# Transform pieces of the last five batches placed by tables of steps, with each piece's PSUM bank written down

## The chip, the cores and the metric

The kernel runs on one core of one Trainium2 chip. A core has five engines with queues of their own: TensorE (PE in the profile; its weight loads are PEld), VectorE (DVE), ScalarE (ACT), GpSimd (POOL) and SyncE (SP), which here only issues DMAs. The metric is the device time of one execution in microseconds (us). Before the change the median of three runs is 810.65 us (809.49 to 811.81).

## What is computed

Each of 8 batches has 3008 rows of 256 channels. A real Fourier transform along the rows, a multiplication with a complex filter and the inverse transform mix the rows; then each row goes through a layer of 2048 hidden channels with a leaky activation that has a slope of its own for each hidden channel.

```python
X = np.fft.rfft(x, axis=1)                      # x: 8 x 3008 x 256
F = (filt_r + 1j * filt_i)[None, :, :]
y = np.fft.irfft(X * F, n=x.shape[1], axis=1)
...
h = y.reshape(24064, 256) @ w_in                # 256 -> 2048
g = np.maximum(h, 0.0) + alpha * np.minimum(h, 0.0)
out = g @ w_out                                 # 2048 -> 256
```

## The kernel before

**The layer.** The rows of a pair of batches (6016) are cut into 12 blocks of 512 (the sixth has 384), so there are 48 blocks, and each has 16 steps: 768 steps, 96 for a batch. In each step PE does the up product of one group of 128 hidden channels (two matmuls of 512 columns, L414, into one half of a double PSUM tile hps) and one sixteenth of the down product of the block before (four matmuls of 256 columns, three behind the 384 block, L433). After every second step ACT moves both halves of hps to SBUF (gtb, L420), and DVE makes the activation of it in place (two L423, one L424). After every eighth step (phases 7, 15, ... 71, 79, ... of a batch's 96) ACT moves two finished down results to osb (L438), and SP stores them with two or three DMAs (L396).

**The transform.** It is split in two factors, 3008 = 47 x 64, and done by small pieces that are put between the steps. For one batch b there are

- 16 pieces A: one matmul of 512 columns (L164), moved by ACT to asb (L238). After every fourth one save_a lets SP store a quarter of asb to DRAM (a_dram, L169). turn_a then loads all of it back in another layout, as at (four DMAs in steady state, L176; their lines of DRAM are 512 bytes).
- 12 pieces B: two matmuls (L184) from at. DVE reads their PSUM tile twice, with two copies of the filter (ww L188, uu L189), and POOL issues two DMAs that swap the halves of ww's partitions into sw (L191).
- 12 pieces S: DVE adds sw to uu (L196).
- 12 pieces C: two matmuls (L209) from uu, moved by ACT to v. After every third one turn_c lets SP store a quarter of v to DRAM (v_dram, four DMAs, L218). After the last it also loads zt, the whole in another layout, in four quarters (L224).
- 16 pieces D: four matmuls of 94 columns (L231) from zt, four pieces to a quarter; ACT moves them to yT, from which the up products read.

x is loaded by POOL (load_x, L128), each quarter of the next batch at a step that the plan gives.

**Order.** The kernel sets the order of all instructions itself (a manual schedule): what is called first stands first in each engine's queue. `plan` maps a step to calls; before the up product of each step, the calls that were put at this step run, those of lower batches first. For b = 3 to 7, plan_fft sets everything from p = 96 (b - 1): A at p - 68 + 2.4 i, turn_a at p - 27, B at p + 5, 9, 15, 19, 25, ..., S 8 steps and C 12 steps after B, D at p + 91 to 95 and then every second step to p + 117. Below, a phase is the step minus p; piece A of batch b + 1 at p' - 27 is phase 69 of batch b, as p' = p + 96.

**PSUM.** Of the eight banks four belong to hps, two to the down products and two to the transform's pieces. These two are one pool (psF, L96), which gives them out in turn: every piece A, B, C or D takes the bank that the piece before the last had, and its first matmul waits until ACT, or for a B DVE, has read that.

```python
def bank(wide=False):
    if wide:
        return psH.tile([128, 2, 512], FP32, name="hps")[:, 0]
    return psF.tile([128, 512], FP32, name="psF")
```

Other buffers on the way have one copy (asb, at, v, zt), three (ww, sw, osb) or four (uu, x).

Of the kernel before, what the change touches and what calls it, by code (L numbers as in the profile page):

```python
# [11 lines left out]
FP32 = mybir.dt.float32  # L12
# [6 lines left out]
NB = 8  # L19
DFF = 2048  # L20
NH = 32
AF = mybir.ActivationFunctionType
OP = mybir.AluOpType

# [40 lines left out]
def kernel(  # L65
# [10 lines left out]
    nc = tc.nc  # L76
# [16 lines left out]
    p_osb = ctx.enter_context(tc.tile_pool(name="p_osb", bufs=3))  # L93
    psH = ctx.enter_context(tc.tile_pool(name="psH", bufs=2, space=bass.MemoryType.PSUM))
    psO = ctx.enter_context(tc.tile_pool(name="psO", bufs=2, space=bass.MemoryType.PSUM))
    psF = ctx.enter_context(tc.tile_pool(name="psF", bufs=2, space=bass.MemoryType.PSUM))  # L96
    dram = ctx.enter_context(tc.tile_pool(name="dram", bufs=1, space=bass.MemoryType.DRAM))
    a_dram = dram.tile([NB, 96, NH, D], FP16, name="a_dram")
    v_dram = dram.tile([NB, 96, NH, D], FP16, name="v_dram")
    ctx.enter_context(tc.manual_schedule())  # L100
# [20 lines left out]
    def xrow(b, h, c):  # L121
        return bass.AP(tensor=x.tensor, offset=x.offset + (b * NFFT + NH * h + 8 * c) * D,
                       ap=[[N2 * D, N1], [1, 8 * D]])

    def load_x(b, c):
        xs = p_x.tile([2 * N1, 8 * D], FP16, name="xs")
        for h in range(2):
            nc.gpsimd.dma_start(out=xs[h * N1 : h * N1 + N1], in_=xrow(b, h, c))  # L128
        return xs

    def load_filt(dst, pbase, src, ka, kb):
# [7 lines left out]
            in_=bass.AP(tensor=src.tensor, offset=src.offset + (N1 - ka) * D,  # L139
                        ap=[[47 * D, 32], [-D, n], [1, D]]))  # L140

    def bank(wide=False):
        if wide:
            return psH.tile([128, 2, 512], FP32, name="hps")[:, 0]
        return psF.tile([128, 512], FP32, name="psF")


    class Fft:
# [5 lines left out]
        def start_a(self):  # L154
            self.asb = p_fft.tile([96, NH, D], FP16, name="asb")
            self.at = p_fft.tile([128, NK1, D], FP16, name="at")

        def piece_a(self, i, evict, wide=False):
            if i == 0:
                self.start_a()  # L160
            xs = xc[(self.b, i // 4)]
            ps = bank(wide)
            o = (i % 4) * 512
            nc.tensor.matmul(ps[0:96], wf1_s, xs[:, o : o + 512], start=True, stop=True)  # L164
            evict(self.asb[:, 2 * i : 2 * i + 2].rearrange("p a d -> p (a d)"), ps[0:96])
# [5 lines left out]
        def turn_a(self, eng, ka=0, kb=NK1):  # L171
            for h in range(2):
                for c in range(2):
                    r = h * 48 + c * NK1
                    q = c * 64 + NH * h
                    eng.dma_start(  # L176
                        out=self.at[q : q + NH, ka:kb],
                        in_=a_dram[self.b, r + ka : r + kb].rearrange("k s d -> s k d"))

        def piece_b(self, kp):  # L180
            px = bank().rearrange("p (k d) -> p k d", k=2)
            for kh in range(2):
                k1 = 2 * kp + kh
                nc.tensor.matmul(px[:, kh], twf_s[:, k1], self.at[:, k1], start=True, stop=True)  # L184
            uu = p_uw.tile([128, 2, D], FP16, name="uu", bufs=4)
            ww = p_uw.tile([128, 2, D], FP16, name="ww")
            sw = p_uw.tile([128, 2, D], FP16, name="sw")
            nc.vector.tensor_mul(ww, px, filts_s[:, 2 * kp : 2 * kp + 2])  # L188
            nc.vector.tensor_mul(uu, px, filt_s[:, 2 * kp : 2 * kp + 2])  # L189
            for o in (0, 64):  # L190
                nc.gpsimd.dma_start(out=sw[o : o + 64], in_=ww[64 - o : 128 - o])  # L191
            self.uw[kp] = uu, sw
# [6 lines left out]
        def piece_c(self, kp, evict, pv=None):  # L199
            if kp == 0:  # L200
                self.v = p_fft.tile([128, NK1, D], FP16, name="v")
                self.zt = p_fft.tile([96, NH, D], FP16, name="zt")
            us = self.uw.pop(kp)
            if pv is None:
                pv = bank().rearrange("p (k d) -> p k d", k=2)
            for kh in range(2):
                k1 = 2 * kp + kh
                for u in us:
                    nc.tensor.matmul(pv[:, kh], twi_s[:, k1], u[:, kh], start=u is us[0], stop=u is us[-1])  # L209
            evict(self.v[:, 2 * kp : 2 * kp + 2], pv)  # L210
# [26 lines left out]
    def on_act(o, i):  # L237
        nc.scalar.activation(o, i, AF.Copy)  # L238

# [75 lines left out]
    xc = {(0, c): load_x(0, c) for c in range(4)}  # L315
# [88 lines left out]
    class Block:  # L404
# [4 lines left out]
        def up(self, j):  # L409
# [6 lines left out]
            if j % 2 == 1:  # L416
                g = gtb[:, turn[0] % 17]
                turn[0] += 1
                m = p_m.tile([128, 2, 512], FP16, name="m")
                nc.scalar.activation(g[:, :, 0:tn], self.hps[:, :, 0:tn], AF.Copy)  # L420
                for i in range(2):
# [5 lines left out]
        def down(self, q):  # L427
            n = self.tn // 128
            for w in range(n * q, n * (q + 1)):
# [5 lines left out]
                if k == 15 and (si % 2 == 1 or si == n - 1):  # L435
                    m = si % 2 + 1
                    osb = p_osb.tile([128, 2, D], FP32, name="osb")
                    nc.scalar.activation(osb[:, 0:m], self.op[:, 0:m], AF.Copy)  # L438
                    for lane in range(m):
# [4 lines left out]
    def put(step, fn, *args):  # L444
        plan.setdefault(step, []).append((fn, args))

    def plan_fft(b, a0, ga, ta, b0, gap, add, lag, d0, quarters, x_at):
        f = Fft(b)
        for i in range(16):
            put(int(a0 + ga * i), f.piece_a, i, on_act)  # L450
        for c in range(4):
            put(int(a0 + ga * (4 * c + 3)), f.save_a, c)
            if b + 1 < NB:
                put(x_at[c],
                    lambda b=b, c=c: xc.update({(b + 1, c): load_x(b + 1, c)}))
        for q in range(quarters):
            w = NK1 // quarters
            put(ta, f.turn_a, nc.sync, w * q, w * q + w)
        bs = [b0 + (2 * int(gap * kp / 2) if add else int(gap * kp)) for kp in range(12)]
        for kp in range(12):  # L460
            put(bs[kp], f.piece_b, kp)
            if add:
                put(bs[kp] + add, f.piece_s, kp)
            put(bs[kp] + lag, f.piece_c, kp, on_act)
        for q in range(4):
            put(bs[3 * q + 2] + lag + 1, f.turn_c, q)
        for i in range(16):
            put(d0 + min(i, 4) + 2 * max(i - 4, 0), f.piece_d, i, on_act)
# [13 lines left out]
    plan_fft(2, 66, 2, 97, 109, 4.5, 8, 12, 187, 4, (110, 114, 118, 122))  # L482
    for b in range(3, NB):
        p = 96 * (b - 1)
        plan_fft(b, p - 68, 2.4, p - 27, p + 5, 5, 8, 12, p + 91, 1, (p + 6, p + 10, p + 16, p + 20))

    prev = None
    step = 0
# [43 lines left out]
```

## Time and profile before

The profiled execution has a span of 805.5 us; the median of the runs is 810.65. The table cuts the span where steps 192, 288, 384, 480, 576 and 672 begin, so each middle row is one batch's 96 steps; busy times are in us.

| stretch, us | length | PE | DVE | ACT | share of the DMA engines |
|---|---|---|---|---|---|
| 0 to 37.6 (loads, first transform) | 37.6 | 29.8 | 23.4 | 19.7 | 1.02 |
| 37.6 to 236.0 (steps 0 to 191) | 198.4 | 192.7 | 162.4 | 154.1 | 0.65 |
| 236.0 to 331.4 | 95.4 | 94.6 | 79.3 | 73.6 | 0.56 |
| 331.4 to 427.4 | 96.0 | 94.5 | 80.0 | 75.0 | 0.56 |
| 427.4 to 522.8 | 95.4 | 94.6 | 79.3 | 73.7 | 0.56 |
| 522.8 to 618.8 | 96.0 | 94.5 | 80.0 | 75.0 | 0.55 |
| 618.8 to 709.0 (no piece A left) | 90.2 | 90.0 | 78.7 | 66.2 | 0.35 |
| 709.0 to 805.5 | 96.5 | 90.8 | 63.9 | 61.8 | 0.15 |

How to read it: matmuls are pipelined and their ends are modelled, so short waits of PE hide in its busy time; the times between the starts of matmuls show them better. The granted clock of TensorE is full from 5.4 us to the end of the work. Profile lines name a line of the kernel, an engine, an operation and the tiles (out<-in), with buffer numbers left out.

### The profile page before, as it was taken

The page shows a single profiled execution, that of the slowest core. Times are in us where ns is not written, and L with a number is a line of the kernel's source. Part 1 is how long each engine was busy: PE and PEld are TensorE (multiplying, and loading weights), DVE is VectorE, ACT ScalarE, POOL GpSimd, SP SyncE. Part 2 cuts the span into 40 slices and gives each one's busy share as a digit, 9 for nine tenths or more (in the row PEclk, how much of TensorE's full clock was granted, in tenths as well). Part 3 has the DMA queues.
Part 4 walks back from the last instruction along what each step waited for, and adds up shares of the span by engine and source line. Part 5 has one row for each costly group of instructions (what it writes and reads, how often), then busy time and mean ns, then how long its engine had stood idle before and what let it go on. Part 6 is the DMA issues. An engine that isn't in the chain of part 4 may idle for free.

```text
span 805.5 us, 16163 instructions
## 1 busy us (share of the span) xinstructions
PE 781.5 (97%) x5980; PEld 538.6 (67%) x5980; DVE 647.0 (80%) x1449; ACT 599.1 (74%) x836; POOL 140.4 (17%) x269
## 2 busy tenths in 40 slices
PE   6999999999999999999999999999999999999997
PEld 5756666666666666766667666766666666776665
DVE  4797985899879897798878888798877999777773
ACT  3788677878778777877868877787877867696663
POOL 7410330232004220131102321032200222000000
PEclk9999999999999999999999999999999999999999
DMA  9977457674756446574484543854465233511111
GB/s 187 199 146 207 106 133 176 185 153 120 166 135 125 110 128 149 138 142 112 112 200 99 113 126 104 211 110 112 114 160 141 53 97 85 134 40 34 41 40 53
DMA packets 94247, 100.59 MB, mean 125 GB/s; under 512 B 11320, under 2 KB 81992, under 8 KB 94040
## 3 DMA queue, kind: packets, MB, share of 16 engines
q1 hardware_dynamic: 79512, 68.80, 32.3%
q0 software_dynamic: 14656, 30.75, 20.1%
q8 instruction: 47, 0.77, 0.4%
q14 instruction: 32, 0.26, 0.1%
HBM read 56.26 MB, written 46.66 MB: 128 GB/s over the span
## 4 chain that ended last, share of the span: by engine, by line
PE 74%; DVE 12%; ACT 7%; issue 3%; DMA 3%; SPq 1%; POOL 0%; ACTq 0%; DVEq 0%; POOLq 0%
PE op L433 32%; PE hps L414 31%; ACT gtb L420 4%; DVE m L423 4%; DVE gtb L424 3%; PE psF L209 3%; PE psF L164 2%; DVE ww L188 2%; DVE uu L189 2%; PE psF L231 2%; PE psF L184 1%; ACT asb L238 1%; DMA xs<-in_x_dram 1%; DMA v_dram<-v 1%; ACT osb L438 1%
## 5 line engine op out<-in xcount | busy, mean ns | idle before, releaser
L420 ACT ACTIVATE gtb<-hps 128x1024 f16<-128x1024 f32 (+1 forms) x384 | 385.4, 1004 | 111.2 <-PE hps L414 110.6
L433 PE MATMUL op<-wout_s,gtb 128*128 128x256 f16 x3008 | 451.1, 272 | 0.6 <-DVE gtb L424 0.6
L414 PE MATMUL hps<-yT,win_s 128*128 128x512 f16 (+1 forms) x1536 | 449.1, 374 | 0.4 <-ACT gtb L420 0.2
L433 PEld LDWEIGHTS <-gtb 128*128 128x128 f16 x3008 | 293.3, 98 | 189.5 <-DVE gtb L424 0.9
L423 DVE TENSOR_SCALAR m<-gtb,alm_s 128x512 f16<-128x512 f16 (+1 forms) x768 | 237.7, 351 | 108.1 <-ACT gtb L420 107.3
L424 DVE TENSOR_TENSOR gtb<-gtb,m 128x1024 f16<-128x1024 f16 (+1 forms) x384 | 261.6, 681 | 24.3 <-PE hps L414 0.5
L191 POOL DMA_DIRECT2D sw<-ww x168 | 87.7, 527 | 503.1 <-DVE ww L188 494.1
L414 PEld LDWEIGHTS <-win_s 128*128 128x128 f16 x1536 | 146.1, 98 | 31.1 <-issue 3.1
L238 ACT ACTIVATE yT<-psF 128x376 f16<-128x376 f32 x120 | 58.2, 485 | 25.4 <-PE psF L231 25.1
L238 ACT ACTIVATE asb<-psF 96x512 f16<-96x512 f32 x112 | 66.1, 591 | 12.4 <-PE psF L164 12.0
L238 ACT ACTIVATE v<-psF 128x512 f16<-128x512 f32 x84 | 50.2, 597 | 29.3 <-PE psF L209 28.9
L438 ACT ACTIVATE osb<-op 128x512 f32<-128x512 f32 x96 | 56.3, 586 | 6.1 <-issue 3.2
L188 DVE TENSOR_TENSOR ww<-psF,filts_s 128x512 f16<-128x512 f32 x84 | 57.4, 684 | 0.1
L189 DVE TENSOR_TENSOR uu<-psF,filt_s 128x512 f16<-128x512 f32 x84 | 57.2, 682 | 0.0
L164 PE MATMUL psF<-xs,wf_s 94*96 94x512 f16 x112 | 43.1, 385 | 1.7 <-ACT v L238 1.0
L231 PE MATMUL psF<-wi_s,zt 96*128 96x94 f16 x504 | 41.9, 204 | 2.5 <-DMA zt<-v_dram 1.6
L231 PEld LDWEIGHTS <-zt 96*128 96x128 f16 x512 | 35.4, 97 | 7.3 <-DMA zt<-v_dram 1.9
L128 POOL DMA_DIRECT2D xs<-in_x_dram x64 | 34.8, 555 | 25.6 <-PE psF L164 13.3
L209 PE MATMUL psF<-uu,twi_s 128*128 128x256 f16 x168 | 33.7, 274 | 4.9 <-DVE uu L189 4.5
L184 PE MATMUL psF<-at,twf_s 128*128 128x256 f16 x168 | 32.1, 272 | 0.2
L196 DVE TENSOR_TENSOR uu<-uu,sw 128x512 f16<-128x512 f16 x72 | 30.1, 418 | 0.0
L209 PEld LDWEIGHTS <-twi_s 128*128 128x128 f16 x192 | 16.7, 98 | 12.8 <-DVE uu L189 10.2
(57 smaller groups left out, 191.3 us busy)
## 6 DMA issues: line engine op xcount, KB each, us to landing
out_dram<-osb SPq DMA_DIRECT2D x128, 128.0 KB
xs<-in_x_dram POOLq DMA_DIRECT2D x64, 188.0 KB, 4.4
a_dram<-asb SPq DMA_DIRECT2D x28, 384.0 KB
sw<-ww POOLq DMA_DIRECT2D x168, 64.0 KB, 2.1
v_dram<-v SPq DMA_DIRECT2D x112, 96.0 KB
zt<-v_dram SPq DMA_DIRECT2D x28, 384.0 KB
at<-a_dram SPq DMA_DIRECT2D x20, 384.0 KB
at<-a_dram SPq DMA_DIRECT2D x32, 96.0 KB
```

Source lines behind the costliest of these rows:

```text
L188: nc.vector.tensor_mul(ww, px, filts_s[:, 2 * kp : 2 * kp + 2])
L189: nc.vector.tensor_mul(uu, px, filt_s[:, 2 * kp : 2 * kp + 2])
L191: nc.gpsimd.dma_start(out=sw[o : o + 64], in_=ww[64 - o : 128 - o])
L209: nc.tensor.matmul(pv[:, kh], twi_s[:, k1], u[:, kh], start=u is us[0], stop=u is us[-1])
L231: nc.tensor.matmul(ps[:, m], self.zt[:, 8 * g + 4 * mh + m, dh * 128 : dh * 128 + 128], wi3_s, start=True, stop=True)
L238: nc.scalar.activation(o, i, AF.Copy)
L414: nc.tensor.matmul(self.hps[:, j % 2, 0:tn], win_s[:, kt, j * 128 : (j + 1) * 128], yT[:, kt, self.t0 : self.t0 + tn], start=(kt == 0), st ...
L420: nc.scalar.activation(g[:, :, 0:tn], self.hps[:, :, 0:tn], AF.Copy)
L423: nc.vector.tensor_scalar(m[:, i, 0:tn], g[:, i, 0:tn], 0.0, a, OP.min, OP.mult)
L424: nc.vector.tensor_add(g[:, :, 0:tn], g[:, :, 0:tn], m[:, :, 0:tn])
L433: nc.tensor.matmul(self.op[:, si % 2], self.gts[k][:, 128 * si : 128 * si + 128], wout_s[:, k], start=(k == 0), stop=(k == 15))
L438: nc.scalar.activation(osb[:, 0:m], self.op[:, 0:m], AF.Copy)
```

## The change

For b = 3 to 7 ("four to eight" counted from one) plan_fft is no longer called; five tables give the step of each piece relative to p. The two PSUM banks become two pools of one bank each, and a string of 440 digits says for every piece of the whole kernel, in the order of the calls, which of the two it takes. In most places the digits still alternate. Batches 0, 1 and 2 keep their steps. What is loaded and stored stays, as do its steps for x.

```diff
+BANKS = (
+    "010101010101010101010101010101001011100011011010100100100101010101010101010101010101010101010101"
...
+)
+STEPS_A = (-66, -63, -63, -62, -60, -54, -51, -48, -44, -43, -40, -38, -36, -31, -28, -27)
+STEPS_B = (-7, 1, 7, 19, 25, 28, 35, 41, 48, 54, 59, 64)
+STEPS_S = (1, 9, 15, 28, 39, 33, 47, 46, 55, 63, 65, 69)
+STEPS_C = (10, 19, 28, 39, 46, 46, 54, 62, 63, 67, 71, 74)
+STEPS_D = (89, 90, 92, 93, 95, 97, 99, 102, 105, 108, 110, 111, 118, 120, 123, 134)
...
-    psF = ctx.enter_context(tc.tile_pool(name="psF", bufs=2, space=bass.MemoryType.PSUM))
+    psF = [ctx.enter_context(tc.tile_pool(name=f"psF{i}", bufs=1, space=bass.MemoryType.PSUM)) for i in range(2)]
...
+    order = iter(BANKS)
...
-        return psF.tile([128, 512], FP32, name="psF")
+        return psF[int(next(order))].tile([128, 512], FP32, name="psF")
...
-        plan_fft(b, p - 68, 2.4, p - 27, p + 5, 5, 8, 12, p + 91, 1, (p + 6, p + 10, p + 16, p + 20))
+        f = Fft(b)
+        for i in range(16):
+            put(p + STEPS_A[i], f.piece_a, i, on_act)
+            if i % 4 == 3:
+                put(p + STEPS_A[i] + 1, f.save_a, i // 4)
+        if b + 1 < NB:
+            for c in range(4):
+                put(p + (6, 10, 16, 20)[c], lambda b=b, c=c: xc.update({(b + 1, c): load_x(b + 1, c)}))
+        put(p + STEPS_A[15] + 4, f.turn_a, nc.sync)
+        for kp in range(12):
+            put(p + STEPS_B[kp], f.piece_b, kp)
+            put(p + STEPS_S[kp], f.piece_s, kp)
+            put(p + STEPS_C[kp], f.piece_c, kp, on_act)
+            if kp % 3 == 2:
+                put(p + STEPS_C[kp] + 1, f.turn_c, kp // 3)
+        for i in range(16):
+            put(p + STEPS_D[i], f.piece_d, i, on_act)
```

In phases of a batch, these steps go from the old place to the new one:

| step | before | after |
|---|---|---|
| D0, first piece from zt | 91 | 89 |
| D15, the last one | 117 | 134 |
| last C (C11) / its v stores and the zt loads | 71 / 72 | 74 / 75 |
| last A of the next batch / its asb store / its at load | 64 / 64 / 69 | 69 / 70 / 73 |
| B0 of the next batch (first reader of at) | 101 | 89 |
| least and greatest distance from B to its S | 8 / 8 | 5 / 14 |
| least and greatest distance from B to its C | 12 / 12 | 10 / 21 |

In SP's queue, the two or three output stores of phase 71 stood between the four at loads and the four v stores; after the change they stand ahead of the at loads, and the v stores follow the at loads directly.

## The prediction

> **What bounds the kernel now.** First the page: which engine has no slack. Then the stretches of one batch (96 steps): how much of each is waiting. Then the waits of a stretch, and the timeline at one of them. Last SP's queue around the point where one batch's transform ends and the next one's begins, and the chain of waits at the one place where that queue was late.
>
> ```profile
> span 805.5 us, 16163 instructions
> PE 781.5 (97%) x5980; PEld 538.6 (67%) x5980; DVE 647.0 (80%) x1449; ACT 599.1 (74%) x836; POOL 140.4 (17%) x269
> ```
>
> ```profile
> 331.40:427.40 96.00, 94.52 (x691) 63.45 (x688) 80.00 (x180) 75.01 (x105) 16.84 (x32) 1.00 0.56 131
> 427.40:522.80 95.40, 94.59 (x707) 65.02 (x705) 79.29 (x181) 73.65 (x105) 16.81 (x32) 1.00 0.56 133
> ...
> 800.50:804.00 3.50, 0.00 (x0) 0.00 (x0) 0.00 (x0) 0.59 (x1) 0.00 (x0) 1.00 0.36 100
> 804.00:805.50 1.50, 0.00 (x0) 0.00 (x0) 0.00 (x0) 0.00 (x0) 0.00 (x0) 0.53 0.00 0
> ```
>
> PE is the bound. In these stretches (length, then busy us of PE, PEld, DVE, ACT, POOL, then granted clock) PE is busy to about 1%, and matmul ends are modelled, so I count from starts: two up matmuls follow each other after 216 ns, down ones after 109, those of a piece A after 216, B and C 109, D 41. Steps 384 to 479 hold 80 full steps of 2 x 216 + 4 x 109 = 868 ns, 16 of the 384 wide block of 2 x 163 + 4 x 109 = 762 ns, and 16 A (3.5 us), 12 B (2.6), 12 C (2.6) and 16 D (2.6): 92.9 us. The stretch takes 95.4, so 2.5 us are waits. The same sum leaves 2.5, 3.1, 2.5, 3.1 and 0.7 us for the five stretches from step 192 to 671: 11.8 us, and nothing more, is what a better placing of these pieces can win. Who waits:
>
> ```profile
> PEld L209 <- DVE uu L189: 1.9, 5, 0.6
> PEld L164 <- DVE uu L189: 0.9, 3, 0.3
> PE psF L209 <- DVE uu L189: 0.7, 3, 0.3
> ```
>
> ```profile
> 372.24 0.68 DVE L188 TENSOR_TENSOR ww<-psF,filts_s 128x512 f16<-128x512 f32 x1
> ...
> 372.84 0.68 DVE L189 TENSOR_TENSOR uu<-psF,filt_s 128x512 f16<-128x512 f32 x1
> ...
> 373.58 0.39 PE L209 MATMUL psF<-uu,twi_s 128*128 128x256 f16 x2 [0.34 <-DVE uu L189]
> ```
>
> It is the PSUM bank: a C or A piece whose bank the B piece two steps earlier still holds, until DVE has read it twice. By the records, a bank is free again 2.3 to 2.9 us (median 2.5) after a B starts, 1.0 to 1.8 (1.27) after an A, 1.03 after a C, 0.85 after a D. Two steps with one piece between are 2.2 us: eight such places a batch, 0.15 to 0.9 us each.
>
> ```profile
> 399.41 1.23 SPq L396 DMA_DIRECT2D out_dram<-osb  x2
> 400.74 0.54 SPq L169 DMA_DIRECT2D a_dram<-asb  x1
> 404.18 2.43 SPq L176 DMA_DIRECT2D at<-a_dram  x4
> 407.07 2.53 SPq L396 DMA_DIRECT2D out_dram<-osb  x3
> 409.64 2.62 SPq L218 DMA_DIRECT2D v_dram<-v  x4
> 415.69 1.73 SPq L224 DMA_DIRECT2D zt<-v_dram  x4
> 417.46 4.66 SPq L396 DMA_DIRECT2D out_dram<-osb  x5
> ```
>
> ```profile
> 130.16 1.88 DMA v_dram<-v
> ...
> 132.19 4.41 DMA zt<-v_dram
> ...
> 136.64 0.34 PE psF L231 x4
> ```
>
> SP here serves b=4's end (v out, zt back) and b=5's beginning (asb out, at back). By their landings, the four at loads come one after another, 1.8 us apart: 407.9, 409.8, 411.9, 413.6. The three out stores and four v stores issued behind them land behind them, at 414.0 to 414.6 and 414.8 to 415.6: the transfers go in the order of issue. zt waits for v (415.69), its first quarter lands at 419.4, and b=4's D0 starts at 422.2: 2.8 us to spare. For b = 2, 3, 5, 6 and 7 the same reading gives 3.4, 1.4, 0.8, 3.3 and 3.7. The second fence is b=1, where zt was late: PE stood 1.9 us.
>
> **The change, part by part.** No engine gets more or fewer instructions.
>
> *Bank waits, removed.* In the new tables, from step 192 on, no piece follows a B on its bank by less than 2.7 us of PE work (3.0 at all but two places), so the waits on B go: -11.8 us.
>
> *Bank waits, added.* What remains are same-bank neighbours one step apart: A at phase 34 after A at 33 (1.09 us), C at 46 after A at 45 (1.31), B at 54 after A at 53 (1.31). Against an A's 1.0 to 1.8 us that is 0 to 0.7 us each; with most releases at 1.1 to 1.3 I take 0.3 + 0.15 + 0.15 for each of b = 3 to 6, and 0.8 at step 211, where a B has the bank of a C in the same step (0.22 of 1.03 us): +3.2 (bounds 0 and 7). Before step 192 the banks change and b=3's A pieces mix with b=2's B and C, with waits of 0.1 to 0.6 us on both sides: 0 (-1 to 1).
>
> *S and the partition swap.* S comes 5 steps after its B at the closest (8 before). The swapped copy landed 4.4 to 7.8 us after the B started, mostly near 5, and S ran 9 to 10 us after it for 7.5 us of steps, so DVE lags about 2: five steps are 4.6 + 2 = 6.6 us. DVE would rarely wait, and it has 17 us of slack in a batch. 0.
>
> *The transposes through DRAM, moved.* C11 goes from phase 71 to 74, its v stores from 72 to 75, b's D0 from 91 to 89; b+1's last A from 64 to 69, its asb store from 64 to 70, its at load from 69 to 73. On SP, the stores of the output block that ends in phase 71 used to stand between at and v; now at follows them and v follows at directly. Worked for b=4, from its step at phase 69, 402.9 in this trace:
> - three steps with the A and a C: phase 72 at 402.9 + 3.05. The output stores start 1.4 us after phase 72 begins (405.7 to 407.07 above) and take 2.5: SP is free at 409.9. The asb store, 2.6 us after its A (398.11 to 400.74) and 3.4 to land, was done at 408.9.
> - at is issued at 409.9 instead of 404.2. Its last quarter lands 9.4 later (404.18 to 413.55): 419.3.
> - v's packets are queued behind. They took 1.1 us after the output stores (414.6 to 415.6): 420.4. zt issues 0.1 later, and its first quarter lands 3.8 after that: 424.3, a rounded 424.4.
> - D0's place is 20 steps and three pieces after phase 69: 402.9 + 18.0 = 420.9. PE stands 3.4 us, and nothing fills it: everything behind D0 on PE is in order.
> The same with their own rows: b=6 3.4, b=3 3.2, b=5 3.1 (only two output stores, but nine short steps ahead of D0), b=2 1.3 (its D0 stays, but b=3's at is issued 5.7 later). b=7 has no at behind it: v stores 0.9 after phase 75, 5.0 to land, 4.0 for zt is 9.9 against 11.2 us to D0: 0. Together +14.4. Bounds: +19 if v needs the 2.1 us that it needs from at's landing to its own with stores between, +5 if two microseconds of each are made up by an earlier at. Behind the late D0 wait B0 of b+1 (at landed at 419.3, no wait of its own) and the up matmuls; the next D quarters need zt quarters 1.3 to 1.5 us apart and come six steps later. On SP the output stores of phases 79 and 87 wait behind zt as before, some 5 us longer; osb has three copies and the next one is written in phase 95, so ACT doesn't wait. On POOL the x loads (phases 6 to 20) stand between swaps as before, and the xs they overwrite were read by phase -27: 0.
>
> Sum: 805.5 - 11.8 + 3.2 + 14.4 = 811.3 of span. The median of the runs (810.65) lies 5.15 above this execution's span, so 816.
>
> A price that the sum leaves out is the clock. Rows: it is granted in full 2.7 us after the first matmul (matmuls 107 ns apart until 5.38, 56 after), it stayed full over the 1.9 us of b=1, and it fell to half at 804.1, 3.7 us after the last matmul ended. The four waits of 3.1 to 3.4 lie between. The Trainium skill (TensorE: Matmul & The Clock Gate, "What's actually happening") has the clock fall after an idle window of about 3.4 us, free-running, and rise after as long a busy one; this trace's 3.7 and 2.7 us agree roughly, and by the page's figure each fall would cost an estimated 1.7 us.
>
> **The rivals.** *Zt comes in time (faster).* If the v stores overtake the at loads, or at is issued before the output stores, zt lands as in b=7, 11.6 us after v's step (689.0 to 700.6), against 11.2 or 12.2: waits under 0.5. Then 805.5 - 11.8 + 3.2 + 0.5 x 4 = 798.9, so 804 (802 with none). For: slack of up to 3.4 us before. Against: the landings above, strictly in order of issue. It decides where the D0 waits together stay under 6.
>
> *The clock falls in the D0 waits.* Each costs 2.7 us at half rate, 1.35 lost, four times 5.4: 821. For: 3.4 is near 3.7. Against: 1.9 did nothing, and these waits are shorter than the only one that did.
>
> *The bank waits only move.* A in pairs (phases 33, 33, 34 and 52, 53) load ACT with 0.6 us evictions next to a 1.02 us one, and B at 25 and 28 put 2.7 us on DVE in three steps; if the releases grow by as much as the old waits, 805.5 + 14.4 + 5.15 = 825. Against: ACT is busy 75 of 96 us, and hps waits are 0.1 us per 48 steps now.
>
> **How the numbers follow.** Late zt as worked: 0.62, 816, and its own range 809 to 821. Zt in time: 0.17, 804. Falling clock: 0.12, 821. Moved bank waits: 0.09, 825. Leaving out half of the first rival and the far end of the last, 8 in 10 lie in 804 to 823. No change means within 0.3%, 808.2 to 813.1, which is what a measurement here can tell: a quarter of the first case, 0.16, as the D0 waits may be 3 to 8 us less than worked. Faster: 0.17 and a little of the first, 0.19. Slower: 0.65.
>
> **What would show it.** In the new profile the chain of waits has zt<-v_dram ahead of D0 for b = 3 to 6, with PE idle some 3 us each, at issued after the stores of phase 71, v landing about a microsecond behind at; the DVE releases of C and A are gone, and the stretches between D0s hold at most 1 us of waits. I'm wrong if zt lands before phase 89, if D0 waits sum to under 6 us, or if the granted clock dips.

## The result, and the profile after

The changed kernel is slower: 820.83 us (816.49 to 821.55, 4 runs) against 810.07 for the kernel before in the same comparison, a ratio of 1.0125 (95% interval 1.0095 to 1.0155). The profiled execution took 821.07 us with a span of 819.2, 13.7 above the span before.

The page, and the stretches of batch 4's and batch 5's 96 steps (columns: length, busy PE, PEld, DVE, ACT, POOL, granted clock, share of the DMA engines, GB/s). All lines of the code have moved down by 14 or so: L164 is L178, L231 is L245, L414 is L428.

```profile
span 819.2 us, 16110 instructions
...
PE 784.6 (96%) x5980; PEld 543.9 (66%) x5980; DVE 646.6 (79%) x1449; ACT 598.6 (73%) x836; POOL 139.5 (17%) x269
...
PE 79%; DMA 9%; ACT 5%; DVE 3%; SPq 2%; issue 1%; POOL 1%; ACTq 0%; DVEq 0%; POOLq 0%
```

```profile
337.10:436.30 99.20, 95.04 (x690) 64.42 (x688) 80.10 (x181) 74.76 (x105) 16.66 (x32) 0.98 0.53 126
436.30:533.90 97.60, 95.19 (x707) 66.22 (x706) 79.26 (x181) 73.74 (x105) 16.67 (x32) 0.98 0.54 130
```

A batch takes 97.6 to 99.2 us where it took 95.4 or 96.0, and the clock is no longer full in it. DMA is 9% of the chain that ended last; before the change it was 3%:

```profile
PE 74%; DVE 12%; ACT 7%; issue 3%; DMA 3%; SPq 1%; POOL 0%; ACTq 0%; DVEq 0%; POOLq 0%
```

The waits say where (longest in total; the lines that name the transform's PE pieces and the partition swap):

```profile
PEld L245 <- DMA zt<-v_dram: 16.8, 6, 4.4
PE psF L245 <- DMA zt<-v_dram: 15.1, 6, 4.1
...
DVE uu L210 <- DMA sw<-ww: 3.1, 1, 3.1
...
PE psF L223 <- DVE uu L203: 1.7, 1, 1.7
```

C waiting for DVE, the wait that the tables were to spread away, is left at one place. D waiting for zt has come. SP's queue at the end of batch 4, and the end of the chain there:

```profile
406.28 0.31 SPq L183 DMA_DIRECT2D a_dram<-asb  x1
409.64 2.19 SPq L410 DMA_DIRECT2D out_dram<-osb  x3
411.95 2.71 SPq L190 DMA_DIRECT2D at<-a_dram  x4
414.70 3.53 SPq L232 DMA_DIRECT2D v_dram<-v  x4
423.41 1.73 SPq L238 DMA_DIRECT2D zt<-v_dram  x4
```

```profile
417.93 5.41 DMA v_dram<-v
423.41 4.05 DMA zt<-v_dram
427.51 0.34 PE psF L245 x4
```

at is issued behind the output stores. By the landing records its last quarter is there at 421.3, v at 423.3, the first quarter of zt at 427.5. D0 could have started at 423.3: PE stood 4.2 us. After it the matmuls of a down step follow each other after 213 ns instead of 109. The time line cut at the steps of the clock:

```profile
424.46:427.87 3.41, 0.36 (x6) 0.35 (x7) 0.17 (x1) 0.00 (x0) 0.00 (x0) 1.00 0.95 257
427.87:431.28 3.41, 3.41 (x17) 1.91 (x16) 2.45 (x5) 1.99 (x3) 1.03 (x2) 0.50 0.98 279
431.28:434.70 3.42, 3.42 (x31) 2.42 (x30) 1.46 (x4) 2.34 (x4) 0.00 (x0) 1.00 0.31 110
```

The clock goes to half for one stretch of 3.41 us, about when PE starts again: 17 matmuls start in it, and 31 in the equal stretch behind. This happens once for each of b = 3, 4, 5 and 6. Less the 0.9 us in which PE still waited, 12.7 us at half rate are 6.3 us lost.

The whole difference, from the starts of matmuls in both traces:

| term | forecast, us | measured, us |
|---|---|---|
| old waits of steps 192 to 671 | -11.8 | -11.8 |
| bank and other waits left there | +3.2 | +4.6 |
| D0 waiting for zt, b = 2, 3, 4, 5, 6 | 1.3, 3.2, 3.4, 3.1, 3.4: +14.4 | 2.0, 2.7, 4.2, 2.5, 3.0: +14.4 |
| half clock after four of these | 0 (rival: 5.4) | +6.3 |
| start of step 0 | 0 | +0.4 |
| span | 811.3 | 819.2 (the rows sum to 819.4) |

### The profile page after: what moved, and what is told of

Same layout as the page of the kernel before. It is cut to its first block, busy times and chain, and to the rows that moved or that the text cites. A ratio compares the mean times of both kernels' runs of the same rounds, so it can differ in the third digit from the quotient of the medians.

```text
span 819.2 us, 16110 instructions
## 1 busy us (share of the span) xinstructions
PE 784.6 (96%) x5980; PEld 543.9 (66%) x5980; DVE 646.6 (79%) x1449; ACT 598.6 (73%) x836; POOL 139.5 (17%) x269
## 4 chain that ended last, share of the span: by engine, by line
PE 79%; DMA 9%; ACT 5%; DVE 3%; SPq 2%; issue 1%; POOL 1%; ACTq 0%; DVEq 0%; POOLq 0%
PE hps L428 34%; PE op L447 33%; DMA v_dram<-v 4%; DMA zt<-v_dram 3%; PE psF L178 3%; PE psF L245 3%; ACT gtb L434 3%; PE psF L223 2%; PE psF L198 2%; SPq L232 2%; DMA xs<-in_x_dram 1%; ACT asb L252 1%; DMA sw<-ww 1%; DVE m L437 1%; PE hps L295 1%
## 5 line engine op out<-in xcount | busy, mean ns | idle before, releaser
L428 PE MATMUL hps<-yT,win_s 128*128 128x512 f16 (+1 forms) x1536 | 452.0, 376 | 0.4 <-ACT gtb L434 0.2
L428 PEld LDWEIGHTS <-win_s 128*128 128x128 f16 x1536 | 145.3, 99 | 31.7 <-issue 3.9
L252 ACT ACTIVATE asb<-psF 96x512 f16<-96x512 f32 x112 | 65.8, 591 | 10.2 <-PE psF L178 10.2
L245 PE MATMUL psF<-wi_s,zt 96*128 96x94 f16 x504 | 43.1, 208 | 16.0 <-DMA zt<-v_dram 15.1
L245 PEld LDWEIGHTS <-zt 96*128 96x128 f16 x512 | 35.9, 100 | 22.5 <-DMA zt<-v_dram 16.8
L178 PE MATMUL psF<-xs,wf_s 94*96 94x512 f16 x112 | 42.0, 381 | 1.6 <-ACT v L252 0.7
L223 PEld LDWEIGHTS <-twi_s 128*128 128x128 f16 x192 | 18.5, 98 | 5.9 <-issue 1.8
```

The costliest lines, as they stand in the source:

```text
L245: nc.tensor.matmul(ps[:, m], self.zt[:, 8 * g + 4 * mh + m, dh * 128 : dh * 128 + 128], wi3_s, start=True, stop=True)
L428: nc.tensor.matmul(self.hps[:, j % 2, 0:tn], win_s[:, kt, j * 128 : (j + 1) * 128], yT[:, kt, self.t0 : self.t0 + tn], start=(kt == 0), st ...
```

## The experiments

Theory: at, issued late, holds up v and zt behind it in one queue; D0 waits for that at a place fixed by its step; the waits let the clock fall. Rivals: 15 steps from C11 to D0 are too few in themselves; the slow matmuls are a cause of their own; the digits carry the gain; spread pieces cost PE elsewhere. In each kernel with another order of pieces the digits are set anew for that order. Every ratio is to the kernel before, run beside it (medians of 808.3 to 809.6 us there), so ratios compare better than times do.

**e5_after, the changed kernel again** next to e6 and e7.

> The changed kernel once more, beside the kernels it is compared with. Both theories: ratio 1.010 to 1.016 to the kernel before; D0 waits of 2 to 4.5 us for b = 3 to 6 and one window of 3.4 us at half clock after each that leaves most of a window idle, so that the runs differ by how many windows fall (about 1.6 us each).

823.66 us (820.64 to 825.1), ratio 1.0180 (1.0160 to 1.0199), so somewhat worse than the first time, and than expected. In its profile D0 waits 3.0, 4.0, 3.5 and 3.3 us (b = 3 to 6), and the clock falls after two of these only, and once after b = 1's D0, which waits 2.4 us at step 92, ahead of all steps that the change moves. So the number of falls differs from run to run, and "one after each" was wrong. It is taken up in the last section.

**e1_fill, matmuls in the wait.**

```diff
+            for _ in range(FILL.get(self.b, 0) if i == 0 else 0):   # FILL = {3: 40, 4: 60, 5: 40, 6: 45}
+                nc.tensor.matmul(pd[:, 0:128], id16, id16, start=True, stop=True)
```

> The changed kernel, but the wait for zt ahead of D0 of b = 3, 4, 5 and 6 is filled with 40, 60, 40 and 45 matmuls of 128 columns (2.2, 3.4, 2.2 and 2.5 us at 56 ns each) into D0's own PSUM tile, which D0 then overwrites. Theory (the D0 waits cost 14.4 us, and the half clock after four of them another 6.3): zt lands when it did, the clock stays full, D0 follows at once or under 0.9 us later, and the time falls by 6 to 7 us, to 814 or 815. Rival (the clock has another cause, or the slow matmuls after D0 cost nothing): within 2 us of the changed kernel, or 9 us above it if the fill adds to the wait.

816.87 us (816.82 to 819.13), ratio 1.0109 (1.0082 to 1.0137). Against the changed kernel's two ratios, 1.0125 and 1.0180, that is some 1 and 6 us less, and only the second difference is clear of the intervals; 6 to 7 were expected. In the profile the clock doesn't fall once before the end (granted 0.997 to 1.0 in all four runs, 0.986 to 0.995 in the eight runs of the changed kernel). PE at batch 4's D0:

```profile
420.97 3.51 PE L246 MATMUL psF<-id 128*128 128x128 f16 x60
425.41 0.34 PE L248 MATMUL psF<-wi_s,zt 96*128 96x94 f16 x4 [0.92 <-DMA zt<-v_dram]
```

The 60 matmuls run, then D0 waits on. Fill and rest come to 3.5, 4.5, 3.6 and 4.5 us for b = 3 to 6, so zt's lateness was 3.7 us more in all than in the changed kernel's first profile and 2.3 more than in its second (13.8). Of the 6.3 us that full clock saves, this takes 3.7 back; step 192 begins 1.6 sooner here (236.9 against 238.5), and that makes the 4.2 between the spans of the two profiles (815.0 against 819.2). The fill removes the falls, as the theory says; that it doesn't itself delay zt isn't excluded by one profile.

**e3_at_behind, the at load put behind v and zt.**

```diff
-        put(p + STEPS_A[15] + 4, f.turn_a, nc.sync)
+        put(p + STEPS_A[15] + 8, f.turn_a, nc.sync)
```

> The changed kernel with the at load put at p' - 19 (phase 77) instead of p' - 23, so that SP issues it behind the v stores and the zt loads of the batch before. Theory (transfers go in the order of issue on one queue): D0 no longer waits, as in b = 7, zt's first quarter landing some 10 us after the v stores' step; at lands some 8 us later than B0 wants it, so the wait moves to B0 and grows, clock falls remain, 835 to 850 us. Rival (zt is slow for a reason of its own, such as 512-byte lines of v): D0's wait stays at 2 us or more.

853.55 us, ratio 1.0556 (1.0512 to 1.0600), above the 835 to 850 expected. SP's queue at batch 4's end, and the longest wait of a B:

```profile
425.77 2.21 SPq L232 DMA_DIRECT2D v_dram<-v  x4
429.79 1.72 SPq L238 DMA_DIRECT2D zt<-v_dram  x4
431.55 8.18 SPq L190 DMA_DIRECT2D at<-a_dram  x4
```

```profile
PE psF L198 <- DMA at<-a_dram: 32.8, 4, 8.7
```

From the first v store to zt's issue it is now 4.0 us, where it was 8.7 with at ahead. No D0 of b = 3 to 6 waits over 0.25 us. The B0 of all five batches waits 8.0 to 8.9 us for at instead. It settles the main point: the v stores weren't slow, they stood behind at. The rival is out, and so is the one that 15 steps from C11 to D0 are too few in themselves: they are the same here.

**e2_a_early, the last A pieces earlier.**

```diff
-STEPS_A = (-66, -63, -63, -62, -60, -54, -51, -48, -44, -43, -40, -38, -36, -31, -28, -27)
+STEPS_A = (-66, -63, -63, -62, -60, -54, -51, -48, -44, -43, -40, -38, -36, -34, -33, -31)
```

> The changed kernel with the last three pieces A at p - 34, -33 and -31 (before -31, -28, -27); asb's last store and the at load follow at the same distances, so at is issued ahead of the output stores of phase 71 again; the bank digits from step 192 on are set anew for the new order. Theory (D0 waits because the v stores queue behind an at load that starts too late): at issued 4 to 5 us earlier in each batch, D0 waits of 0 to 0.5 us, no half clock, 800 to 803 us. Rival (15 steps from C11 to D0 are too few in themselves): D0 still waits 2 us or more in each batch, 812 us or above.

809.22 us (807.13 to 811.76), ratio 1.0014 (0.9998 to 1.0030): between the two forecasts, and not to be told from the kernel before. Most of the loss is gone, but not all: D0 waits 3.2, 1.6, 1.6 and 0.4 us, and after the first of these the clock falls. SP's queue again, batch 4:

```profile
402.05 2.22 SPq L232 DMA_DIRECT2D v_dram<-v  x4
404.37 0.51 SPq L183 DMA_DIRECT2D a_dram<-asb  x1
407.86 2.46 SPq L190 DMA_DIRECT2D at<-a_dram  x4
410.42 3.24 SPq L410 DMA_DIRECT2D out_dram<-osb  x3
413.70 2.28 SPq L232 DMA_DIRECT2D v_dram<-v  x4
```

What the expectation left out: asb's store now comes behind the v stores of C8 (phase 64), which hold SP until 404.27; the store is issued 3.9 us after its A instead of the 2.6 reckoned, and at follows it. at gained about 3 us of 4 to 5. The direction is the theory's; a queue that an earlier step is moved into had to be counted too.

**e6_d_late, the first D pieces later.**

```diff
-STEPS_D = (89, 90, 92, 93, 95, 97, 99, 102, 105, 108, 110, 111, 118, 120, 123, 134)
+STEPS_D = (93, 93, 94, 95, 95, 97, 99, 102, 105, 108, 110, 111, 118, 120, 123, 134)
```

> The changed kernel with D0 to D3 at 93, 93, 94 and 95 (before 89, 90, 92, 93) and D4 at 95 as there; the bank digits from step 192 on are set for the new order. Everything ahead of D0 is untouched, so zt lands when it did. Theory (zt is late against a fixed place on PE, and the up and down steps can run ahead of D0): four steps or 3.3 us of other work stand ahead of D0, its waits fall to 0 to 1.2 us each, no window at half clock, and the time falls by 14 to 18 us from the changed kernel, less up to 3 us that the up product of phase 96 waits for D3's eviction: 801 to 806 us on a chip where the kernel before takes 808. Rival (the wait moves with D0, as zt's transfer or PE's order depends on something at D0): waits stay over 2 us, 815 or more.

802.3 us (799.99 to 805.74), ratio 0.9934 (0.9910 to 0.9958): faster than the kernel before. All else as in the changed kernel: at still goes ahead of v, and zt lands as late. But up and down products stand ahead of D0, which waits 0.5 (with the piece behind it), 0.8, 0.2 and 1.2 us for b = 3 to 6. Batch 4's stretch:

```profile
330.90:424.90 94.00, 93.39 (x691) 63.77 (x689) 80.09 (x180) 74.47 (x105) 16.66 (x32) 1.00 0.56 133
```

94.0 us against 99.2, with full clock. The first four D places cost the changed kernel all that it won, and more.

**e9_alt_late and e4_alt, the digits.** In e9 the digits alternate from the 88th piece on, in e4 from the first.

> The changed kernel with its own first 87 digits, which are the banks that the kernel before had in the same places, and strict alternation for the other 353. Theory (e4_alt lost its extra time in batch 1's first pieces, and the digits are worth little once the steps are spread): within 2 us of the changed kernel, 818 to 824 us. Rival (the written digits carry the gain): 3 us or more above it.

820.09 us, ratio 1.0139 (1.0113 to 1.0166): no difference from the changed kernel that can be told. In its trace C waits for DVE at five places, 2.8 us in all, where the changed kernel has one place and 1.7 us.

> The changed kernel with the bank digits strictly alternating, as the one pool gave the banks out before. Theory (the waits for banks left with the spread steps, not with the digits; same-bank distances are nearly the same either way): within 2 us of the changed kernel, D0 waits as there. Rival (the written digits are what removes the bank waits): 3 to 8 us slower than it, with waits of C and A on DVE back.

824.83 us (823.37 to 831.33), ratio 1.0228 (1.0177 to 1.0279): not within 2 us. The first 48 steps, e4 and then the changed kernel:

```profile
37.20:90.10 52.90, 47.38 (x343) 30.64 (x343) 42.10 (x92) 38.73 (x56) 6.55 (x13) 1.00 0.67 156
```

```profile
38.00:88.30 50.30, 47.09 (x342) 30.69 (x342) 41.97 (x92) 38.38 (x56) 7.15 (x13) 1.00 0.71 165
```

2.6 us go there: three A pieces of batch 1 wait 1.0 to 1.1 us for their bank. The kernel before has no such waits and takes 49.8 us for these steps, so its pool can't alternate there. As built, its first 87 pieces have the banks of the digits; no trace shows a bank's number. So the sentence further up that the pool gives the banks out in turn holds only roughly, and the digits there keep what was. Beyond them they are worth about 1 us of waits in e9's trace and nothing that its time shows; the spread steps are what removed most of the bank waits.

**e7_both, other tables with the old ends.**

```diff
+STEPS_A = (-67, -64, -63, -62, -60, -53, -49, -47, -46, -44, -40, -38, -36, -34, -33, -32)
+STEPS_B = (-6, 3, 7, 16, 21, 26, 35, 41, 46, 53, 57, 61)
+STEPS_S = (2, 11, 15, 24, 29, 34, 43, 49, 54, 61, 65, 68)
+STEPS_C = (14, 23, 27, 38, 44, 51, 55, 59, 66, 67, 69, 71)
+STEPS_D = (91, 92, 93, 94, 97, 98, 101, 102, 105, 106, 107, 114, 115, 118, 124, 135)
```

> Tables of the same kind with the old ends: last A at phase 64, its store at 65 ahead of the v stores of C8, at load at 68, C11 at 71, D0 at 91, S 7 or 8 steps after its B; spacing in between chosen by the same-bank distances (1.2 us or more after an A, 3 after a B at nearly all places), digits to match. Theory (spreading is worth the 11.8 us of bank waits, and the changed kernel lost them, and more, at the transposes): D0 waits under 1 us in all, no half clock, bank waits of 1 to 4 us left, so 8 to 10 us below the kernel before: 798 to 801 on a chip where that takes 808. Rival (spread pieces cost PE elsewhere, in ACT or DVE backlogs): 804 or more.

802.96 us (801.43 to 804.5), ratio 0.9928 (0.9913 to 0.9942). The stretches of b = 4 and 5:

```profile
333.20:427.70 94.50, 94.14 (x691) 63.87 (x690) 79.79 (x181) 74.29 (x105) 16.76 (x32) 1.00 0.55 133
427.70:521.90 94.20, 94.00 (x707) 65.32 (x705) 79.04 (x181) 73.08 (x105) 16.66 (x32) 1.00 0.56 134
```

No D0 of b = 2 to 7 waits over 0.35 us, but 5.6 us of small waits are left in steps 192 to 671 (11.8 before), mostly 0.2 us each of an A, a C or a D. So the tables gain 6, not 8 to 10. It beats both kernels as e6 does, and the two can't be told apart.

**e8_fill_b1, e7 with b = 1's wait filled** and D0 to D3 a step later.

> e7_both with D0 to D3 one step later (92 to 95) and 28 matmuls of 128 columns (1.6 us) ahead of b = 1's D0, whose zt is late in every kernel here (1.3 to 2.35 us). Theory (the clock falls where PE idles 2.3 us or more within one fixed window of 3.41 us, and b = 1's wait is at that edge): the idle part of that wait goes under 1 us, the clock is full in every run, the time stays where e7_both was at full clock, 800 to 802 us, and the spread between runs falls from 3 us to 1 or 2. Rival (the spread comes from elsewhere): granted clocks under 0.997 still turn up.

802.28 us (801.2 to 804.2), ratio 0.9915 (0.9892 to 0.9937). The profiled run has full clock throughout, but two of six runs show 0.993 and 0.997, so the spread did not go. Where the clock fell in these two isn't known; only one run has a profile.

## Why the prediction was right, and where it was off

Right, in its direction and by its main step: the order of transfers on SP. at starts behind the output stores, v behind at, zt behind v, and D0, two steps earlier, meets a zt that is late; the five waits are each within 0.9 of what was worked. That their sum came out at 14.4 as well is luck: single waits are off by -0.6 to +0.8, and in the second profile the five come to 15.5. For b = 4 the step most off is the stores of v, which landed 2.0 us behind at (421.3 to 423.3), not 1.1; the prediction had that in its upper bound alone. e3 shows the queueing, e6 that D0's place decides. The old waits of C and A on DVE left as reckoned (-11.8). B0's wait for at didn't show, nor one in ACT, osb or the xs loads.

Three terms were off. *The clock.* The prediction kept it out of the sum, as a rival with 0.12 at 821, because "these waits are shorter than the only one that did". It came true, on top of the forecast, and is the one step that failed, by the prediction's own sign of being wrong, "if the granted clock dips". Half clock cost 6.3 us where the sum had 0 and the rival 5.4: waits of 2.5 to 4.2 us were enough, and an idle time of 3.4 us isn't needed. e1 shows that filling the waits removes the falls.

*S and the swap*, put at 0. At one place C3 of b = 7 waited 1.8 us for its bank, which B6 held until DVE had read it; and DVE had stood 3.1 us in S5, 5 steps after B5, for the swap (the DVE line above). POOL had issued that swap some 3 us late (665.19, where B5's ww had ended at 661.97). The kernel before has a wait of the same kind (6.0 us of POOL behind DVE's gtb, against 6.3), where 8 steps covered it. In e7, with 7 or 8 steps, POOL has one such wait too (7.9 us behind DVE's m), but no S waits for the swap. Why POOL is late there stays open.

*The offset from span to median*, put at 5.15, is 1.6 here. Each run lies 1.7 to 1.9 above its own span; the profiled execution of before was a fast one among its runs (805.5, where the spans of its runs in the later comparisons go from 804.9 to 809.4). So, by luck, 3.5 us too much here hid part of what was missing elsewhere (6.3 for the clock, 1.4 for the waits left): 816 and 820.8 are nearer to each other than the steps are.

## What to carry to other kernels

Before a consumer is moved earlier or a producer later, read the queue that joins them, with everything that the same move pushes ahead of it: here five steps fewer between the last C and D0, and a load of the next batch that now goes ahead, turned 0.8 to 3.3 us of slack (b = 3 to 6) into waits of 2.5 to 4.2. In these runs a wait of PE of 2.5 us could cost 1.7 us of half clock on top of its length, and four steps of other work in front of it (e6) took most of it away. Space pieces by how long each holds its buffer (2.5 us for a B, 0.9 to 1.3 for the others); which of two buffers each gets then hardly matters.

## What the runs showed of the hardware

The clock is judged in fixed windows. In the first trace it fell at 328.88, 427.87, 526.86 and 622.43 us: the distances are 29, 29 and 28 times 3.413 us, and it stayed at half for exactly one such window. In all eleven traces every later change of the clock is a whole number of such windows after the first. Laying this grid over them, and taking PE's busy time as lines like those above show it: half clock followed every window of full clock in which PE was busy for 1.31 us or less (idle for 2.10 or more), and none in which it was for 1.53 or more (idle for 1.88 or less). The window nearest to the edge, from e9, with the one behind it, and then the nearest on the other side, from e4:

```profile
522.24:525.65 3.41, 1.31 (x16) 1.11 (x17) 1.11 (x3) 0.87 (x2) 0.00 (x0) 1.00 1.02 279
525.65:529.07 3.42, 3.42 (x22) 2.26 (x19) 1.81 (x5) 1.61 (x3) 1.04 (x2) 0.50 1.00 298
```

```profile
622.21:625.62 3.41, 1.53 (x12) 0.88 (x9) 2.20 (x5) 1.51 (x2) 0.00 (x0) 1.00 0.60 171
625.62:629.03 3.41, 2.25 (x22) 1.67 (x23) 1.45 (x3) 1.71 (x3) 0.67 (x2) 1.00 1.01 247
```

So it depends on where a wait lies. Here are a wait of 2.50 us in the changed kernel's first profile, nearly all in one window, and one of 3.28 us in its second, cut in 1.54 and 1.74:

```profile
523.45:526.86 3.41, 1.08 (x13) 0.88 (x13) 1.27 (x4) 0.78 (x3) 0.00 (x0) 1.00 0.99 274
526.86:530.27 3.41, 3.41 (x19) 2.25 (x17) 1.88 (x5) 1.70 (x3) 1.03 (x2) 0.50 0.99 302
```

```profile
618.96:622.37 3.41, 1.96 (x15) 1.13 (x12) 2.62 (x6) 1.51 (x2) 0.00 (x0) 1.00 0.44 110
622.37:625.78 3.41, 1.74 (x18) 1.31 (x19) 1.15 (x2) 1.20 (x2) 0.16 (x1) 1.00 1.04 284
625.78:629.19 3.41, 3.41 (x32) 2.40 (x31) 2.62 (x7) 2.66 (x6) 0.88 (x2) 1.00 0.87 271
```

The first pair falls to 0.50, the longer wait leaves 1.00. The Trainium skill (TensorE: Matmul & The Clock Gate, "What's actually happening") has a free-running window of 3413 ns, which these traces confirm (3.413), and a fall after an idle window of about 3.4 us; here a window that was idle for six tenths of its length was enough. In the five waits of 8 to 9 us of e3 the half clock lasted longer: 10.2 us, three windows, from 231.1, 337.0, 545.2 and 647.6, and 6.8 us, two windows, from 442.8. PE was idle through all or nearly all of the first of these windows, and each time the clock rose at the end of the first one that PE worked through.
